# Shared staging rows, later parameter turns, and transfers over 128 partitions with the token group outermost

## The chip, the cores and the metric

One core of a Trainium2 chip runs the whole program: TensorE (PE, with its weight loads PEld), VectorE (DVE), ScalarE (ACT), GpSimd (POOL) and SyncE (SP), and sixteen DMA engines that all queues share. DMAs are issued by SP, ACT and POOL, each in its own order. The metric is the device time of one execution in microseconds. Before the change the median of three runs is 953.67 us (948.99, 953.67, 957.39).

## What is computed

Forward and backward of a gated mix of two branches over L = 2048 tokens of D = 448 channels, all in bf16. `u` is the input, `G` the gradient of the output:

```python
g = sigmoid((u * gate_w).sum(-1, keepdims=True))
a = S4(u)      # y = irfft(rfft(u, 2L) * rfft(K, 2L))[:L] + u * Dskip,  K[d, l] = Re sum_n C dB exp(dt A l)
b = MLP(u)     # relu(u @ w1 + b1)**2 @ w2 + b2
out = g * a + (1 - g) * b
# returned: out, and the gradients of u, A, B, C (real and imaginary), log_dt, Dskip, w1, b1, w2, b2, gate_w
```

## The kernel before, in words

The FFTs are matmuls in two steps of 64 with a turn through DRAM between them. Three sequences are transformed forward: `u` into `gd[0]`, `DA = g * G` into `gd[1]` and the convolution kernel into `gd[2]`. Three products are transformed back through `hd[0]`, `hd[1]`, `hd[2]`. A tile framework gives every engine a fixed order of instructions and sets the semaphores; `tc.issue_after(x)` only puts an instruction behind `x` on its own engine.

**Start (0 to 58 us).** `U` and `G` are held as 128 partitions x 16 tokens: partition 32 g + p holds tokens 64 p + 16 g to 64 p + 16 g + 15, for four groups g of 32 partitions. Eight DMAs load `U` (L398 to L401; each one group of 32 partitions, eight tokens or 7,168 B a row), four load `G` (L410, L411; 14,336 B a row), alternating between SP and ACT. Behind them on SP stand six DMA transposes of the parameters (L420 to L422, the "parameter turns"), the constants `M2`, `MI`, `Etw`, `sel`, and three small loads. `fwd1` (L219 to L241) runs eight steps: four matmuls, their evacuation by ACT and DVE into a staging row of [128, 4, 448], and two stores of 224 KB into `gd`, one from POOL (`q2`) and one from SP. `u` rotates through four staging rows in `F17`, `DA` through six in `R32`. Then `s1_load` (L498) reads `gd` back turned and `fwd2` (L247) makes the spectra with `M2`.

**First inverse (58 to 213 us).** `spectrum`, `powers` (L617; it stores its records to `rec_d` from ACT) and `inv1p` fill `hd[0]`. Four calls of `load_hs` (L316) read it back: each reads 896 KB by two DMAs of 64 partitions, one on ACT and one on SP, 256 rows of 1,792 B each. 160 small matmuls (L713) sum them into the gradient of the convolution kernel, which goes to `dk_d` (L726) and comes back as `DK` (L733). Every chunk of the middle part needs `DK`.

**Middle (213 to 630 us).** Fourteen chunks of parameter gradients, with the MLP's matmuls between them.

**End (630 to 946 us).** Row blocks and weight gradients of the MLP (`grad_w2`, `grad_w1`, whose rows POOL loads at L1148), products of spectra, `inv1` into `hd[1]` and `hd[2]`, eight more calls of `load_hs`, all on SP, into a ring of three buffers that also takes the spectra (`load_sx`, on SP too), `inv2` (L322) and the stores of `out` (L1367, from POOL) and of the gradient of `u` (L1391, SP and ACT), four DMAs of 32 partitions for each of four steps. `G` is loaded a second time at L1267.

The lines that say which DRAM dimension is outermost, in `load_hs` and in the store of `dk_d`:

```python
src = bass.AP(tensor=hd, offset=(8 * hp + 2 * q) * D, ap=[[64 * D, 64], [16 * D, 4], [1, 2 * D]])                       # L318
bass.AP(tensor=dk_d, ..., ap=[[st_ * na * D, 16 // st_], [16 * na * D, 4], [1, D]])   # L726; 16 // st_ is 16, for one piece 8
```

Of the kernel before, what the change touches and what calls it, by code (L numbers as in the profile page):

```python
# [163 lines left out]
class Ker:  # L164
    def __init__(self, tc, pool, psum):
        self.tc = tc
        self.nc = tc.nc
        self.pool = pool
        self.psum = psum
        self.evac_i = 0  # L170
        self.st_i = 0
        self.st_more = []
        self.q2 = tc.nc.gpsimd
        self.pair_i = 0
        self.pairs3 = True
        self.act_only = False
        self.stage_i = 0
        self.dma_i = 0
        self.n = 0
# [39 lines left out]
    def fwd1(self, rhs, gd, stage, act_first=0):  # L219
        nc = self.nc  # L220
        for hh in range(2):
            for q in range(4):
                self.act_only = 4 * hh + q < act_first
                st = stage[self.stage_i % len(stage)]
                self.stage_i += 1
                for j2 in range(2):
                    ps = self.pair()
                    for jj in range(2):
                        self.last_f1 = nc.tensor.matmul(ps[jj][:, 0:D], lhsT=self.F1[:, hh * 128:(hh + 1) * 128], rhs=rhs(q * 4 + j2 * 2 + jj), start=True, stop=True)
                    ev = self.evac2(st[:, 2 * j2:2 * j2 + 2, :], ps)  # L230
                    if self.act_only:
                        self.last_ev = ev
                    elif ev.ins.engine == mybir.EngineType.DVE:
                        self.last_dv = ev
                j0base = 32 * hh + q * 4
                for g2 in range(2):
                    dst = bass.AP(tensor=gd, offset=(j0base + 16 * g2) * 64 * D, ap=[[D, 64], [64 * D, 4], [1, D]])
                    d = (self.q2 if g2 == 0 else nc.sync).dma_start(dst, st[g2 * 64:(g2 + 1) * 64])
                    if g2 == 0:
                        last = d  # L240
        return last  # L241

    def load_s1(self, gd, q, s1, queue=None):
# [70 lines left out]
            nc.scalar.dma_start(dst, st[:])  # L314

    def load_hs(self, hd, q, hs, both=False):  # L316
        for hp in range(2):
            src = bass.AP(tensor=hd, offset=(8 * hp + 2 * q) * D, ap=[[64 * D, 64], [16 * D, 4], [1, 2 * D]])  # L318
            last = (self.nc.scalar if both and hp == 0 else self.nc.sync).dma_start(hs[64 * hp:64 * hp + 64].rearrange("p g x d -> p g (x d)"), src)
        return last  # L320

    def inv2(self, hs, q, x, hp, ps, more=()):  # L322
# [12 lines left out]
def kernel(ctx, tc, A_u, A_A_re, A_A_im, A_B_re, A_B_im, A_C_re, A_C_im, A_log_dt, A_Dskip,  # L335
# [31 lines left out]
    K = Ker(tc, pool, psum)  # L367


    def tl(ap2d, g):  # L370
        return bass.AP(tensor=ap2d.tensor, offset=ap2d.offset + 16 * g * D, ap=[[64 * D, 32], [1, LT * D]])

    def flat(ap):
        return ap.rearrange("p t d -> p (t d)")
# [20 lines left out]
    gw_bc = const.tile([P, D], bf16, name="gw_bc")  # L395
    nc.sync.dma_start(gw_bc[:], gate_w.partition_broadcast(P))
    load_const("F1BD", nc.scalar)
    for h in range(2):  # L398
        for g in range(NG):
            src = bass.AP(tensor=u2.tensor, offset=u2.offset + (16 * g + 8 * h) * D, ap=[[64 * D, 32], [1, 8 * D]])  # L400
            (nc.sync if g % 2 == 0 else nc.scalar).dma_start(flat(U[32 * g:32 * g + 32, 8 * h:8 * h + 8]), src)  # L401
    G_.dma_start(bass.AP(tensor=dk_d, offset=512 * D, ap=[[2 * D, 128], [1, 2 * D]]), nc.inline_tensor(np.zeros((128, 2 * D), ml_dtypes.bfloat16), name="c_zero").ap())
    ldb = const.tile([P, D], bf16, name="ldb")
    G_.dma_start(ldb[:], A_log_dt.partition_broadcast(P))
# [2 lines left out]
    G_.dma_start(prow[FT:FT + 3], A_log_dt[0:384].rearrange("(t p) -> t p", p=P))  # L407
    G_.dma_start(prow[FT + 3:FT + 4, 0:64], A_log_dt[384:448].rearrange("(t p) -> t p", p=64))
    G_.dma_start(prow[0:FT], B_b1.rearrange("(t p) -> t p", p=P))
    for g in range(NG):  # L410
        (nc.sync if g % 2 == 0 else nc.scalar).dma_start(flat(G[32 * g:32 * g + 32]), tl(G2, g))  # L411
    prm = K.t("X16", [P, 8192])
    raw = {}
    o = 0
# [1 line left out]
    def carve(n):  # L416
        nonlocal o
        o += n
        return prm[:, o - n:o]
    for nm, src in (("Ar", A_A_re), ("Ai", A_A_im), ("Br", A_B_re), ("Bi", A_B_im), ("Cr", A_C_re), ("Ci", A_C_im)):  # L420
        r = carve(2 * D).rearrange("p (h d) -> p h d", h=2)
        nc.sync.dma_start_transpose(out=r, in_=src)  # L422
        raw[nm] = r
    load_const("M2", nc.sync)
    for nm in ("MI", "Etw", "sel"):
        load_const(nm, nc.sync)
    K.M2, K.MI, K.Et = ct["M2"], ct["MI"], ct["Etw"]
    sel = ct["sel"][:].rearrange("p (k m) -> p k m", k=4)
    DB = K.t("D16", [P, LT, D])
    ident = const.tile([P, P], bf16, name="ident")  # L430
    make_identity(nc, ident[:])
# [10 lines left out]
    K.F1 = ct["F1BD"]  # L442
    RA = K.t("R32", [P, 16384])
    Fs = K.t("F17", [P, 8704])
    stage = [[b[:, 1792 * i:1792 * i + 1792].rearrange("p (a d) -> p a d", d=D) for i in range(k)] for b, k in ((Fs, 4), (RA, 6))]
    K.fwd1(lambda j: U[:, j, 0:D], gd[0], stage[0], 5)
    u_ev, u_dv, u_f1 = K.last_ev, K.last_dv, K.last_f1
    s32 = const.tile([P, LT], fp32, name="s32")
    s_b = const.tile([P, LT], bf16, name="s_b")
    g_b = const.tile([P, LT], bf16, name="g_b")  # L450
# [17 lines left out]
    SB = K.t("S25", [P, 12800])  # L468
    turn = SB[:, 4096:12288].rearrange("p (k a l) -> p k a l", k=4, a=DT)

    def transposed(src, spill):
        nonlocal nti
        for t2 in range(LT // 2):
            ps = K.ps(NT[4 + nti % 2], [P, DT, 2 * P], bf16)
            nti += 1
            for tt in range(2):
                for dt in range(DT):
                    sv = src[:, 2 * t2 + tt, dt * P:dt * P + DSZ[dt]]
                    for h in range(1 if dt < 3 else 2):
                        T_.transpose(ps[64 * h:64 * h + DSZ[dt], dt, tt * P:tt * P + P], sv, ident[:], tile_position=(0, 64 * h))  # L480
            cp = S.copy if t2 % 2 == 0 else V.tensor_copy
            lb, k = t2 // 2, t2 % 2
            cp(turn[:, lb % 3, :, 256 * k:256 * k + 256], ps[:])
            if k == 1:
                G_.dma_start(bass.AP(tensor=spill, offset=lb * P * 2048, ap=[[2048, P], [1, 2048]]), turn[:, lb % 3].rearrange("p a l -> p (a l)"))
# [5 lines left out]
    V.tensor_copy(b1_f[:], ps[:])  # L491
    ld4 = b1_f[:, FT:FT + 4]

    lf1 = K.fwd1(lambda j: DA[:, j, :], gd[1], stage[1])
    SX, SY = prm, K.t("Y16", [P, 8192])
    s1r = [b[:, 3584 * i:3584 * i + 3584].rearrange("p (a d) -> p a d", d=D) for b in (SY, SX) for i in range(2)]

# [55 lines left out]
    for q in range(2):  # L553
        l11 = s1_load(1, q)
    with tc.issue_after(u_f1.ins):
        transposed(U, UT_d)
    for t in range(LT):
        V.tensor_scalar(out=DB[:, t, :], in0=G[:, t, :], scalar1=omg32[:, t:t + 1], scalar2=None, op0=ALU.mult)
    ps = K.ps("S", [P, 512])
# [57 lines left out]
    def powers(gr):  # L617
# [20 lines left out]
        for k in range(NLEV):  # L638
            dst = xs[..., 2] if k == 0 else ys[..., 1] if k == 2 else lx[..., (1, 8, 9, 10).index(k)] if k in (1, 8, 9, 10) else ly[..., k - 3]
            S.copy(dst.rearrange("p c t w -> p t c w"), x)  # L640
            if k < NLEV - 1:
# [5 lines left out]
        nc.scalar.dma_start(bass.AP(tensor=rec_d, offset=4 * gr * P * RS, ap=[[RS, P], [P * RS, nch], [1, RS]]), R)  # L647


    spw = K.t("K28", [P, 4, 4, 2, D])  # L650
# [19 lines left out]
    for q in range(4):  # L670
        if q < 3:
            if q > 0:
                spectrum(0, q + 1)
            ls1 = spectrum(1, q + 1) or ls1
        for h in range(2):
            pr = prd[(2 * q + h) % 3]
            K.cprod(pr, spw[:, 2 * (q % 2) + 1], spw[:, 2 * (q % 2)], h)
            K.inv1p(pr, 2 * q + h, hd[0])
        if q == 0:
            with tc.issue_after(f10.ins):  # L680
                transposed(DB, DBT_d)
        if q < 2:
            powers(q + 2)
    with tc.issue_after(ls1.ins):
# [578 lines left out]
        sx = [load_sx(0, q) for q in range(3)]  # L1263

    Gt = K.t("Y16", [P, LT, D])
    for g in range(NG):
        nc.sync.dma_start(flat(Gt[32 * g:32 * g + 32]), tl(G2, g))  # L1267
    brs = [RT[:, 10752 + 1792 * i:12544 + 1792 * i].rearrange("p (h x d) -> p h x d", h=2, x=2) for i in range(3)]
    nb = 0

# [35 lines left out]
    for j in range(FT):  # L1306
        grad_w2(j)
        if j == 8:
            for g in range(NG):
                with tc.issue_after(last_s1.ins):  # L1310
                    nc.sync.dma_start(U[32 * g:32 * g + 32, :, 0:D], tl(u2, g).rearrange("p (t d) -> p t d", d=D))
    for j in range(JS):
        grad_w1(j, NB)

# [23 lines left out]
    for q in range(4):  # L1338
# [23 lines left out]
        V.tensor_copy(sl(dg_b), sl(dg))  # L1362
        V.tensor_tensor(out=sl(ds_b), in0=sl(dg_b), in1=sl(gp), op=ALU.mult)
        V.tensor_copy(sl(ds32), sl(ds_b))
        for g in range(NG):
            dst = bass.AP(tensor=o0.tensor, offset=o0.offset + (16 * g + 2 * q) * D, ap=[[64 * D, 32], [8 * D, 2], [1, 2 * D]])
            G_.dma_start(dst, ao[32 * g:32 * g + 32].rearrange("p (h x) d -> p h (x d)", h=2))  # L1367
    param_grads(2)
    param_grads(3)
    GU = K.t("K28", [P, LT, D])  # L1370
# [2 lines left out]
    for q in range(4):  # L1373
        hs = hsn
        if q < 3:
            hsn = load_hs(2, q + 1)
        xo = dxq[2 + q] if q < 2 else oq[q - 2]
        for x in range(2):
            ps = K.pair()
            l0l = 2 * q + x  # L1380
            for hp in range(2):
                t = l0l + 8 * hp
                S.activation(dgt[:, hp], ident[:], ACT.Copy, scale=ds32[:, t:t + 1])
            for hp in range(2):
# [4 lines left out]
        for g in range(NG):  # L1389
            dst = bass.AP(tensor=o1.tensor, offset=o1.offset + (16 * g + 2 * q) * D, ap=[[64 * D, 32], [8 * D, 2], [1, 2 * D]])  # L1390
            K.dma().dma_start(dst, xo[32 * g:32 * g + 32].rearrange("p (h x) d -> p h (x d)", h=2))  # L1391
# [50 lines left out]
```

## Time and profile before

| what | value |
|---|---|
| median of three runs | 953.67 us |
| the profiled execution's own time / span | 947.82 / 945.7 us |
| busy: PE / DVE / ACT / POOL | 713.5 / 670.9 / 586.5 / 192.2 us |
| mean granted TensorE clock | 0.836 |
| DMA, mean over the span | 196 GB/s, 184.98 MB |
| issues of `hd` into `R` on SP: count, size, median to landing | 16, 448 KB, 6.0 us |

The page cuts the span into 40 slices of 23.6 us and gives, for each, the busy share of every engine and the mean busy share of the sixteen DMA engines in tenths; the chain of waits goes back from the last instruction to whatever released each step; the view of one source line gives its instructions, their time from issue to landing and who waited for them. "SPq" is the queue of SP's DMA issues.

### The profile page before, as it was taken

The numbers are of one execution on the slowest core, as the hardware profiler recorded it, in microseconds if no ns is written. First come the engines' busy times: TensorE is split into PE (matmuls) and PEld (weight loads), VectorE is DVE, ScalarE is ACT, GpSimd is POOL, SyncE is SP. The second block draws the span as 40 slices with busy tenths as digits, with TensorE's granted clock in tenths as the row PEclk, the third lists the DMA queues.
The fourth block names the chain that finished last, engine by engine and source line by source line (L and its number), as shares of the span: only waits on it lengthen the run. The fifth ranks groups of instructions, "written<-read, shape, count | busy, mean of one in ns | idle before, by whom it ended". The sixth has DMA issues, their size and how long they took to land.

```text
span 945.7 us, 19001 instructions
## 1 busy us (share of the span) xinstructions
PE 713.5 (75%) x7657; PEld 342.6 (36%) x7657; DVE 670.9 (71%) x1152; ACT 586.5 (62%) x936; POOL 192.2 (20%) x327
## 2 busy tenths in 40 slices
PE   3346564635978888887898887988869889768985
PEld 1112221214344443434453443543323245423443
DVE  4388986696399999999887899944248671297800
ACT  3345757825998868789676855655237646437553
POOL 2141000112202121121202311232300022433310
PEclk9687565667969998899957999989968889869999
DMA  8987395896626667444844867279999994889431
GB/s 191 266 254 263 120 354 225 306 309 193 146 62 124 151 143 137 111 110 117 198 85 117 218 149 189 79 193 288 378 295 279 295 292 146 228 236 278 144 110 44
DMA packets 161887, 184.98 MB, mean 196 GB/s; under 512 B 90963, under 2 KB 137464, under 8 KB 160872
## 3 DMA queue, kind: packets, MB, share of 16 engines
q1 hardware_dynamic: 111958, 82.38, 35.2%
q0 software_dynamic: 20480, 61.51, 20.3%
q10 hardware_dynamic: 29362, 39.88, 12.9%
q8 instruction: 60, 0.98, 0.5%
q14 instruction: 27, 0.22, 0.1%
HBM read 90.58 MB, written 73.13 MB: 173 GB/s over the span
## 4 chain that ended last, share of the span: by engine, by line
PE 24%; issue 19%; ACT 18%; DMA 17%; DVE 14%; POOL 5%; SPq 2%; ACTq 1%; POOLq 0%; DVEq 0%
PE psN L1021 4%; PE psF L1159 3%; DMA S<-rT_d 2%; ACT R L917 2%; SPq L422 2%; PE psX L844 2%; POOL dhT_d L1097 2%; ACT S L591 2%; DMA hd<-st 1%; PE psN L584 1%; DMA D<-hd 1%; ACT R L871 1%; DMA out_dram<-S 1%; DMA dk_d<-st 1%; DMA U<-in_A_u_dram 1%
## 5 line engine op out<-in xcount | busy, mean ns | idle before, releaser
L1159 PEld LDWEIGHTS <-S 128*128 128x128 bf16 x448 | 44.2, 104 | 63.0 <-issue 20.5
L933 DVE TENSOR_TENSOR P<-R 128x2048 bf16<-128x2048 bf16 x42 | 49.5, 1217 | 23.5 <-ACT R L917 20.6
L917 ACT CAST R<-psF 128x1024 bf16<-128x1024 f32 x56 | 57.5, 1027 | 11.2 <-PE psF L913 11.2
L1021 PE MATMUL psN<-D,S 128*128 128x448 bf16 x208 | 52.0, 382 | 6.4 <-ACT S L591 6.3
L1159 PE MATMUL psF<-U,S 128*128 128x448 bf16 x224 | 51.4, 380 | 2.1 <-ACT S L1154 2.0
L584 PE MATMUL psN<-S,U 128*128 128x512 bf16 x132 | 41.0, 429 | 8.3 <-ACT F L589 4.7
L913 PE MATMUL psF<-R,S 64*32 64x256 bf16 (+1 forms) x1344 | 38.4, 299 | 8.5 <-DMA R<-Y 3.2
L1084 PE MATMUL psN<-S,U 128*128 128x512 bf16 x126 | 36.9, 410 | 7.5 <-ACT D L1089 6.9
L773 DVE TENSOR_TENSOR X<-X,F 128x512 bf16<-128x512 bf16 (+1 forms) x70 | 37.5, 536 | 4.5 <-ACT F L807 2.6
L207 DVE CAST K<-psN 128x448 bf16<-128x448 f32 x36 | 21.7, 620 | 26.5 <-PE psN L255 26.2
L784 DVE TENSOR_TENSOR K<-K,F 128x2048 bf16<-128x2048 bf16 (+3 forms) x42 | 36.4, 866 | 5.6 <-ACT F L812 4.0
L1153 PEld LDWEIGHTS <-S 128*128 128x128 bf16 x448 | 29.8, 102 | 26.4 <-issue 10.0
L1097 POOL DMA_DIRECT2D dhT_d<-D x28 | 20.2, 722 | 90.8 <-DVE D L1096 90.4
L785 DVE TENSOR_TENSOR F<-K,F 128x2048 bf16<-128x2048 bf16 (+3 forms) x42 | 35.9, 855 | 2.7 <-ACT F L814 2.7
L784 DVE TENSOR_TENSOR Y<-Y,F 128x2048 bf16<-128x2048 bf16 (+3 forms) x42 | 36.3, 864 | 1.6
L774 DVE TENSOR_TENSOR F<-X,F 128x512 bf16<-128x512 bf16 (+1 forms) x70 | 36.9, 527 | 0.6
L787 DVE TENSOR_TENSOR K<-K,F 128x2048 bf16<-128x2048 bf16 (+3 forms) x42 | 36.3, 865 | 1.3
L787 DVE TENSOR_TENSOR Y<-Y,F 128x2048 bf16<-128x2048 bf16 (+3 forms) x42 | 36.3, 864 | 1.3
L785 DVE TENSOR_TENSOR F<-Y,F 128x2048 bf16<-128x2048 bf16 (+3 forms) x42 | 35.9, 854 | 0.2 <-ACT F L814 0.2
L1021 PE MATMUL psN<-S,D 128*128 128x448 bf16 x168 | 35.5, 360 | 0.0
L1354 DVE SCALAR_TENSOR_TENSOR F<-psN,Y 128x448 bf16<-128x448 f32 x16 | 9.9, 618 | 36.1 <-PE psN L329 36.1
L883 ACT COPY M<-psX 128x1024 bf16<-128x1024 bf16 x26 | 26.5, 1018 | 13.7 <-PE psX L882 13.3
(378 smaller groups left out, 1944.1 us busy)
## 6 DMA issues: line engine op xcount, KB each, us to landing
sp<-K ACTq DMA_DIRECT2D x8, 896.0 KB, 6.4
hd<-st ACTq DMA_DIRECT2D x16, 448.0 KB, 3.0
dhT_d<-D POOLq DMA_DIRECT2D x28, 256.0 KB, 5.3
R<-sp SPq DMA_DIRECT2D x8, 896.0 KB, 8.9
S<-rT_d POOLq DMA_DIRECT2D x14, 512.0 KB, 5.2
R<-hd SPq DMA_DIRECT2D x16, 448.0 KB, 6.0
S<-dhT_d POOLq DMA_DIRECT2D x14, 512.0 KB, 4.3
rec_d<-F ACTq DMA_DIRECT2D x2, 1920.0 KB, 9.1
```

Source lines behind the costliest of these rows:

```text
L584: T_.matmul(ps[:], lhsT=w1w[:, dt, j * P:j * P + P], rhs=ub[:, dt], start=(dt == 0), stop=False, skip_group_check=True)
L773: V.tensor_tensor(out=hi4, in0=lo, in1=bcast_dims(pr, [0, (None, n), 1]), op=ALU.mult)
L774: V.tensor_tensor(out=Vv.rearrange("p (x a r) -> p x a r", x=2 * W2, r=2), in0=lo, in1=bcast_dims(pi, [0, (None, n), 1]), op=ALU.mult)
L784: V.tensor_tensor(out=hi, in0=lo, in1=bcast_dims(pr, [0, (None, n // 2), 1]), op=ALU.mult)
L785: V.tensor_tensor(out=Vv.rearrange("p (x a q) -> p x a q", x=rows, q=2), in0=lo, in1=bcast_dims(pi, [0, (None, n // 2), 1]), op=ALU.mult)
L787: return V.tensor_tensor(out=T4[:, :, :, n:2 * n], in0=T4[:, :, :, n:2 * n], in1=V4, op=ALU.add)
L913: T_.matmul(psz[32 * ii:32 * ii + m, t, 256 * s:256 * s + 256], lhsT=DKc[64 * t:64 * t + 64, s, g, 2 * ii:2 * ii + 1 + par].rearrange("p i ...
L917: S.copy(zb[:, :, :, gg].rearrange("p s t n -> p t s n"), psz[:].rearrange("p t (s n) -> p t s n", s=2))
L933: lastp = V.tensor_tensor(out=pr.rearrange("p s t g n -> p s t (g n)"), in0=zv, in1=(xb if r == 0 else rev_dim(xb, 2)), op=ALU.mult)
L1021: lastm = T_.matmul(ps[:, 0:D], lhsT=hblk[j][:, P * tt:P * tt + P], rhs=ws[:, j, :], start=(w == 1 and j == 0), stop=(j == FT - 1))
L1097: G_.dma_start(bass.AP(tensor=dhT_d, offset=2 * p_ * P * L + 512 * lb, ap=[[L, P], [P * L, 2], [1, 512]]), hb)
L1159: lastm = T_.matmul(ps[:, 0:width], lhsT=hh[:, t, :], rhs=(DB2[:, t, :] if w == 0 else U[:, t, 0:D + 1]), start=(t == 0), stop=(t == LT - 1))
```

## The change

1. The two lists of staging rows become one list of ten (four in `F17`, six in `R32`); `u` uses rows 0 to 7, `DA` rows 8, 9 and 0 to 5.
2. The parameter turns and the loads of `M2`, `MI`, `Etw` and `sel` are put behind the last store of `u` on SP.
3. `DA`'s second stores go from SP to ACT (`q3`).
4. `U` is loaded by four DMAs of four tokens over all 128 partitions, `G` by two of eight tokens (both times). `load_hs` uses four DMAs over 128 partitions instead of two over 64; the stores of `out` and of `u`'s gradient use two DMAs of 128 partitions instead of four of 32.
5. The evacuations of `u`'s transposes all go to ACT (they alternated between ACT and DVE), and the four stores of `rec_d` move from ACT to POOL.

```diff
@@ fwd1
-                    d = (self.q2 if g2 == 0 else nc.sync).dma_start(dst, st[g2 * 64:(g2 + 1) * 64])
+                    d = (self.q2 if g2 == 0 else self.q3).dma_start(dst, st[g2 * 64:(g2 + 1) * 64])
@@ load_hs
-        for hp in range(2):
-            src = bass.AP(tensor=hd, offset=(8 * hp + 2 * q) * D, ap=[[64 * D, 64], [16 * D, 4], [1, 2 * D]])
-            last = (self.nc.scalar if both and hp == 0 else self.nc.sync).dma_start(hs[64 * hp:64 * hp + 64].rearrange("p g x d -> p g (x d)"), src)
+        for g in range(4):
+            src = bass.AP(tensor=hd, offset=(2 * q + 16 * g) * D, ap=[[8 * D, 2], [64 * D, 64], [1, 2 * D]])
+            last = (self.nc.scalar if both and g % 2 == 0 else self.nc.sync).dma_start(hs[:, g].rearrange("p x d -> p (x d)"), src)
@@ main function
-    def tl(ap2d, g):
-        return bass.AP(tensor=ap2d.tensor, offset=ap2d.offset + 16 * g * D, ap=[[64 * D, 32], [1, LT * D]])
+    def tl(ap2d, t0, n):
+        return bass.AP(tensor=ap2d.tensor, offset=ap2d.offset + t0 * D, ap=[[16 * D, NG], [64 * D, 32], [1, n * D]])
...
-    for h in range(2):
-        for g in range(NG):
-            src = bass.AP(tensor=u2.tensor, offset=u2.offset + (16 * g + 8 * h) * D, ap=[[64 * D, 32], [1, 8 * D]])
-            (nc.sync if g % 2 == 0 else nc.scalar).dma_start(flat(U[32 * g:32 * g + 32, 8 * h:8 * h + 8]), src)
+    for h in range(4):
+        (nc.sync if h % 2 == 0 else nc.scalar).dma_start(flat(U[:, 4 * h:4 * h + 4]), tl(u2, 4 * h, 4))
...
-    for g in range(NG):
-        (nc.sync if g % 2 == 0 else nc.scalar).dma_start(flat(G[32 * g:32 * g + 32]), tl(G2, g))
+    for h in range(2):
+        (nc.sync if h % 2 == 0 else nc.scalar).dma_start(flat(G[:, 8 * h:8 * h + 8]), tl(G2, 8 * h, 8))
...
-    stage = [[... for i in range(k)] for b, k in ((Fs, 4), (RA, 6))]
-    K.fwd1(lambda j: U[:, j, 0:D], gd[0], stage[0], 5)
+    stage = [... for b, k in ((Fs, 4), (RA, 6)) for i in range(k)]
+    K.fwd1(lambda j: U[:, j, 0:D], gd[0], stage, 5)
+    with tc.issue_after(u_st.ins):       # the turns and M2, MI, Etw, sel, moved here from above
...
-            cp = S.copy if t2 % 2 == 0 else V.tensor_copy
+            cp = cps[t2 % 2]             # (S.copy, S.copy) for U, (S.copy, V.tensor_copy) for DB
...
-    lf1 = K.fwd1(lambda j: DA[:, j, :], gd[1], stage[1])
+    K.q3 = nc.scalar
+    lf1 = K.fwd1(lambda j: DA[:, j, :], gd[1], stage)
+    K.q3 = nc.sync
...
-        nc.scalar.dma_start(bass.AP(tensor=rec_d, ...), R)
+        G_.dma_start(bass.AP(tensor=rec_d, ...), R)
...
-    for g in range(NG):
-        nc.sync.dma_start(flat(Gt[32 * g:32 * g + 32]), tl(G2, g))
+    for h in range(2):
+        nc.sync.dma_start(flat(Gt[:, 8 * h:8 * h + 8]), tl(G2, 8 * h, 8))
...
-        for g in range(NG):
-            dst = bass.AP(tensor=o0.tensor, offset=o0.offset + (16 * g + 2 * q) * D, ap=[[64 * D, 32], [8 * D, 2], [1, 2 * D]])
-            G_.dma_start(dst, ao[32 * g:32 * g + 32].rearrange("p (h x) d -> p h (x d)", h=2))
+        for h in range(2):
+            dst = bass.AP(tensor=o0.tensor, offset=o0.offset + (8 * h + 2 * q) * D, ap=[[16 * D, NG], [64 * D, 32], [1, 2 * D]])
+            G_.dma_start(dst, ao[:, 2 * h:2 * h + 2].rearrange("p x d -> p (x d)"))
...
@@ the same edit at the store of o1, on the queues of K.dma()
```

More of the change, by code (lines that the diff above doesn't have):

```diff
@@ L173, in __init__ @@
         self.q2 = tc.nc.gpsimd
+        self.q3 = tc.nc.sync
         self.pair_i = 0
@@ L237, in fwd1 @@
                     dst = bass.AP(tensor=gd, offset=(j0base + 16 * g2) * 64 * D, ap=[[D, 64], [64 * D, 4], [1, D]])
-                    d = (self.q2 if g2 == 0 else nc.sync).dma_start(dst, st[g2 * 64:(g2 + 1) * 64])
+                    d = (self.q2 if g2 == 0 else self.q3).dma_start(dst, st[g2 * 64:(g2 + 1) * 64])
                     if g2 == 0:
                         last = d
+                    else:
+                        self.last_st = d
         return last
@@ L419, in carve @@
         return prm[:, o - n:o]
[L420 to L428, printed above, removed]
     DB = K.t("D16", [P, LT, D])
@@ L444 @@
     Fs = K.t("F17", [P, 8704])
-    stage = [[b[:, 1792 * i:1792 * i + 1792].rearrange("p (a d) -> p a d", d=D) for i in range(k)] for b, k in ((Fs, 4), (RA, 6))]
-    K.fwd1(lambda j: U[:, j, 0:D], gd[0], stage[0], 5)
-    u_ev, u_dv, u_f1 = K.last_ev, K.last_dv, K.last_f1
+    stage = [b[:, 1792 * i:1792 * i + 1792].rearrange("p (a d) -> p a d", d=D) for b, k in ((Fs, 4), (RA, 6)) for i in range(k)]
+    K.fwd1(lambda j: U[:, j, 0:D], gd[0], stage, 5)
+    u_ev, u_dv, u_f1, u_st = K.last_ev, K.last_dv, K.last_f1, K.last_st
+    with tc.issue_after(u_st.ins):
+        for nm, src in (("Ar", A_A_re), ("Ai", A_A_im), ("Br", A_B_re), ("Bi", A_B_im), ("Cr", A_C_re), ("Ci", A_C_im)):
+            r = carve(2 * D).rearrange("p (h d) -> p h d", h=2)
+            nc.sync.dma_start_transpose(out=r, in_=src)
+            raw[nm] = r
+        load_const("M2", nc.sync)
+        for nm in ("MI", "Etw", "sel"):
+            load_const(nm, nc.sync)
+        K.M2, K.MI, K.Et = ct["M2"], ct["MI"], ct["Etw"]
+    sel = ct["sel"][:].rearrange("p (k m) -> p k m", k=4)
     s32 = const.tile([P, LT], fp32, name="s32")
@@ L469, with transposed @@
     turn = SB[:, 4096:12288].rearrange("p (k a l) -> p k a l", k=4, a=DT)
-    def transposed(src, spill):
+    def transposed(src, spill, cps):
         nonlocal nti
@@ L555 @@
     with tc.issue_after(u_f1.ins):
-        transposed(U, UT_d)
+        transposed(U, UT_d, (S.copy, S.copy))
     for t in range(LT):
@@ L646, in powers @@
                 x, y = y, halves(cur[1 - k % 2])
-        nc.scalar.dma_start(bass.AP(tensor=rec_d, offset=4 * gr * P * RS, ap=[[RS, P], [P * RS, nch], [1, RS]]), R)
+        G_.dma_start(bass.AP(tensor=rec_d, offset=4 * gr * P * RS, ap=[[RS, P], [P * RS, nch], [1, RS]]), R)
     spw = K.t("K28", [P, 4, 4, 2, D])
@@ L680 @@
             with tc.issue_after(f10.ins):
-                transposed(DB, DBT_d)
+                transposed(DB, DBT_d, (S.copy, V.tensor_copy))
         if q < 2:
@@ L1310 @@
                 with tc.issue_after(last_s1.ins):
-                    nc.sync.dma_start(U[32 * g:32 * g + 32, :, 0:D], tl(u2, g).rearrange("p (t d) -> p t d", d=D))
+                    nc.sync.dma_start(U[32 * g:32 * g + 32, :, 0:D], bass.AP(tensor=u2.tensor, offset=u2.offset + 16 * g * D, ap=[[64 * D, 32], [D, LT], [1, D]]))
     for j in range(JS):
@@ L1388 @@
             brq.append(load_br(1, q + 3))
-        for g in range(NG):
-            dst = bass.AP(tensor=o1.tensor, offset=o1.offset + (16 * g + 2 * q) * D, ap=[[64 * D, 32], [8 * D, 2], [1, 2 * D]])
-            K.dma().dma_start(dst, xo[32 * g:32 * g + 32].rearrange("p (h x) d -> p h (x d)", h=2))
+        for h in range(2):
+            dst = bass.AP(tensor=o1.tensor, offset=o1.offset + (8 * h + 2 * q) * D, ap=[[16 * D, NG], [64 * D, 32], [1, 2 * D]])
+            K.dma().dma_start(dst, xo[:, 2 * h:2 * h + 2].rearrange("p x d -> p (x d)"))
     dlog_b = const.tile([P, 4], bf16, name="dlog_b")
```

## The prediction

> **What bounds the kernel now.** I read the table of stretches first, then the chain of waits, then the source lines the change touches. The stretches (us, busy of PE, PEld, DVE, ACT and POOL, granted clock, DMA share, GB/s):
>
> ```profile
> 24.00:58.00 34.00, 16.87 (x98) 7.61 (x99) 16.69 (x38) 15.65 (x27) 6.59 (x11) 0.75 0.96 263
> ...
> 192.00:213.00 21.00, 7.91 (x111) 4.23 (x113) 20.11 (x31) 4.09 (x7) 3.60 (x6) 0.67 0.98 308
> 213.00:260.00 47.00, 35.35 (x491) 19.61 (x488) 24.54 (x36) 35.89 (x52) 11.69 (x19) 0.85 0.64 168
> ...
> 741.00:770.00 29.00, 25.61 (x144) 10.92 (x144) 17.66 (x28) 16.50 (x29) 5.31 (x10) 0.76 0.94 278
> 770.00:812.00 42.00, 38.20 (x285) 21.21 (x283) 12.54 (x13) 21.51 (x32) 8.71 (x17) 0.96 0.62 206
> ...
> 835.00:888.00 53.00, 43.09 (x269) 17.70 (x269) 46.12 (x127) 27.57 (x62) 16.85 (x31) 0.79 0.83 234
> ```
>
> The three places where the change works, the start, the read of `hd[0]` at 192 and the end from 741, have a DMA share of 0.83 to 0.98. There the sixteen DMA engines are the scarce thing. The chain of waits (start, us, what), at the start and at 187:
>
> ```profile
> 19.22 5.42 SPq L422
> ...
> 33.26 3.73 DMA gd<-F
> 37.09 0.92 ACT F L216
> ```
>
> ```profile
> 187.45 4.98 DMA hd<-st
> 193.26 12.35 DMA D<-hd
> ...
> 211.60 11.00 DMA dk_d<-st
> 225.78 6.49 DMA K<-dk_d
> ```
>
> First: `u`'s fifth step waits for a staging row whose store stands behind the turns on SP. The view of the `fwd1` stores says who paid (us, times), and that of `load_hs` whom it held:
>
> ```profile
>   DVE F L207: 14.5, 1
>   ACT F L216: 13.9, 1
> ```
>
> ```profile
>   PEld L713: 19.4, 3
>   PE psN L713: 18.1, 3
> ...
> DMA to landing us min/median/max: 4.8/6.6/14.7
> ```
>
> Second: the read of `hd[0]` (issued at 192.6, last landing at 212.7) holds the sums L713, and they hold `DK`.
>
> **The row that decides.** The trace's semaphore records give the increments that each DMA makes on landing. Nearly all make 16. The two `dk_d` stores on SP whose DRAM pattern begins with 8 (218.1 and 218.8 us; 32 partitions on the SBUF side) make 9, those that begin with 16 make 16, one-row DMAs make 2, and the 14-row store at 939.5 makes 15. So on SP and ACT a short transfer shows one more increment than its outermost count: eight rows outermost are served by eight engines, one by one. The changed patterns begin with 2 (`load_hs`) and with 4 (`U`, `G`, `out`, `u`'s gradient); before, the smallest among them was 32. I take 2 and 4 engines. Which engines these are no record says: the ends are the same ones every time, or a fresh set for each DMA. I take the same ones, since nothing in the trace shows a rotation, and keep the other end as a rival.
>
> The Trainium skill ("DMA: Bandwidth & Descriptors", section "Why a DMA increments its semaphore by 16 and not by 1") says that the engine count is the largest number up to 16 that divides the slowest dimension of both sides, and that SP and ACT use the lowest-numbered ones. The rows agree with the first half; the second no row shows, and with it the first end would hold.
>
> The price of one engine comes from the packet records. Their times add up to the page's DMA share, so an engine serves one packet at a time: at the median 41 ns for 896 B, 74 to 86 ns for 1,792 B (by queue), 144 ns (lowest tenth) for 3,584 B, 272 ns for 7,168 B.
>
> **Part by part.**
>
> *Read of `hd[0]`.* 4 calls x 4 DMAs x 128 packets of 1,792 B on 2 engines is 1,024 packets each, x 74 to 80 ns = 76 to 82 us. SP's half and ACT's half share the two engines, so two queues do not help. `w2`, `UT` and the records use the same engines for some 5 us. From 192.6 + 2.5 to the first byte, the end lies at 271 to 282 instead of 212.7: +58 to +69. DVE (20.1 of 21 us busy) finishes its tables meanwhile, but in 213:260 it is busy 24.5 of 47 us, so finishing early buys little; the hidden layer that fills PE there needs `w1`, queued on SP behind these reads. The `dk_d` stores, 11.0 us beside the weights' loads now, should land some 5 us sooner. I take +60, bounds +50 to +69.
>
> *Reads of `hd[1]` and `hd[2]`.* A call is 4 x 64 packets an engine x 74 to 80 ns = 19 to 20.5 us on two engines; now 6 to 13 us. All eight stand on SP, in one order. The other traffic of 741:888 is, by engine, 27 + 26 + 21 + 44 us of busy share (812:835 has 0.89), less 26 for these reads (16 DMAs x 16 packets x 0.1 us under load) and 11 for the output stores (32 x 4 x 0.087): 81 us, which shares the two engines. With a quarter more for that, 24 us a call. Walking it: call (1,0), issued at 741.4, lands at about 775 instead of 750 (shared fully there), so its `inv2` (754.6 now) moves 21 to 25. Calls (1,1) and (1,2) hide behind `grad_w2`, where PE is busy 38.2 of 42 us. From (1,3) on, five calls follow at 24 us: 862, then 892, 916, 940 and 964, against a last need at 872.5: +90. At 19 us a call it is +65, at 30 us +120. The count confirms it: two engines have 81 + 156 (eight calls) + 19 (`u`'s gradient: 8 DMAs x 32 packets x 74 ns on four engines) = 256 us to carry, where 147 us stood. PE's order is fixed, so the late `grad_w1` steps wait too. I take +90.
>
> *Start.* Removed: the 13.9 us wait, and the turns ahead of `u`'s stores. Added: `U` is 4 x 32 packets x 144 ns = 18.4 us on four engines, all landed by about 24 instead of 15.4; `G` is 2 x 32 x 272 ns = 17.4 us behind it, landed at about 41 instead of 24.5. `u`'s transform then ends near 35 instead of 42.7, but `DA` starts at `G`'s landing, about where it starts now (41.3). On SP the turns now take their 16.5 us (13.1 to 29.7) from about 35, with four of their engines backed up, and `M2` lands at 52 to 58. `fwd2` starts at 57.5 now and needs it: -6 to +10, taken as 0. The gain is there and `G` and the turns are late next.
>
> *Second read of `G`, stores of `out`.* 17.4 us on four engines on SP where some 5 stood, in a stretch with DMA share 0.97: 0 to +13, taken as +4, nearest to the early landing (706) against the need (755). The POOL stores are half as many issues of 0.56 us; POOL's queue made 16 increments for every shape, so its engine count cannot be read: -2 to +5, taken as 0.
>
> *`rec_d` from POOL; `DA`'s stores from ACT; evacuations to ACT.* The landing of `rec_d` (9.07 us in the chain) stays, POOL pays four issues of about 1 us; behind them wait the `DBT_d` stores, which nobody needs soon: -2 to +6, taken as +1. Eight ACT issues of 0.4 us and four copies of 1.02 us fall into ACT's idle time at 57.9 to 68.6 (9.4 us before L539): 0, +3 if uncovered. `powers(0)` now waits for `DA`'s rows in `F17`, as the memsets of `R32` do already (4.0 us before 65.8): 0 to +4, taken as 0.
>
> Sum: 60 + 90 + 0 + 4 + 0 + 1 = +155 on the profiled 947.8, which is 1,103. The median of the runs shown lies 5.9 above the profiled run: 1,109, given as 1,110. Bounds: -10 to +41 from the small parts, +115 to +189 from the reads: 1,059 to 1,184.
>
> **Rivals.**
>
> *Faster: the reads keep sixteen engines or rotate* (0.09). The nine-increment rows are stores; no load with a short outermost count is in the trace. If each load takes fresh engines, four DMAs of 4.9 + 2.4 us in parallel land as now (6.6 at the median), and the start is all that is left: the wait of 13.9 us less the turns behind `u` (16.5 us from about 28 end at 45, `M2` by 50, 7 before 57.5), so -7 to -14: 943. It decides where a call keeps about eight engines or more; with eight, the reads already cost +10 in the first inverse.
>
> *Only the first read costs* (0.08). If the fixed order was set with the long reads in view and puts `grad_w1` ahead of `inv2`, PE's 58 us behind 888 cover most of the end: 5.9 + 947.8 + 60 + 15 = 1,029. Against it: the other loads queue on the same two engines.
>
> *Every wide transfer slows* (0.08). While two engines are backed up, each 16-engine DMA lands with its slowest part; POOL's row loads at L1148 then come late even where PE does not wait for `inv2`, and 30 us a call or more gives +120 to +150 at the end: 1,140 to 1,190.
>
> *Nothing changes* (0.03): gains and losses meet within 1%, about what a measurement of this kernel can tell from no change.
>
> **How the numbers follow.** The main case has 0.72. Its own range is 1,059 to 1,184. To leave out no more than 2 in 10, the range goes down to 1,020 (the second rival) and ends at 1,185. Of the first rival's -7 to -14 a third or more lies within 1% (9.5 us): faster 0.05, within 1% 0.07 with the last rival, slower 0.88.
>
> **What would show it.** Right: `load_hs` DMAs with 3 increments and those of `U` with 5; a stretch of some 60 us with a low DMA share after 192, with PE L713 waiting for `D<-hd` and `P<-hd`; `psN` L329 waiting for `R<-hd` from 850 on; no wait of ACT for `gd<-F` before 40. Wrong: 16 increments there, a landing of `hd` under 10 us, or a DMA share over 0.9 in that stretch.

## The result and the profile after

The changed kernel takes 1148.72 us at the median of four runs (1145.56 to 1152.38) against 952.75 us for the kernel before in the same session (948.99 to 957.39): the ratio is 1.2055, with a 95% interval of 1.199 to 1.2121. The profiled execution took 1149.55 us (span 1147.7), 201.7 us more than the profiled one before. That one lies 4.9 us below the median, so by the medians the change costs 196.0.

The view of `load_hs` first, that is L322 of the changed kernel (operation, tiles, count, then the shortest, median and longest issue in ns, first and last start, and below it who waited, in us and times):

```profile
L322 SPq DMA_DIRECT2D R<-hd x32: 486/4320/8635, 839.8 to 1057.3; - x32
...
L322 SPq DMA_DIRECT2D P<-hd x4: 8734/9114/9153, 219.9 to 247.9; - x4
L322 ACTq DMA_DIRECT2D P<-hd x4: 4202/9156/15267, 220.0 to 248.7; - x4
...
  PE psN L717: 77.4, 8
  ACT F L818: 61.0, 1
  PE psN L332: 42.5, 9
  ACT S L1158: 23.7, 1
```

The same view of the kernel before, L319:

```profile
L319 SPq DMA_DIRECT2D P<-hd x2: 587/624/661, 193.9 to 194.5; - x2
...
  PE psN L713: 18.1, 3
  PE psN L329: 2.5, 1
```

Two things are to be seen. The sums (L717, L713 before) now wait 77.4 us for `hd[0]`, where they waited 18.1, and the second inverse (L332) 42.5 us for the later calls, where it waited 2.5. And the *issue* of one such DMA holds SP or ACT for some 9.1 us from the third of each queue on, up to 15.3, where it took 0.6 to 0.85. The trace's records give each DMA 3 increments; they give those of `U`, `G` and `u`'s gradient 5, and those of `out`, issued by POOL, 16.

The table of stretches (us, busy of PE, PEld, DVE, ACT and POOL, granted clock, DMA share, GB/s) has the start, the read of `hd[0]`, what follows it, and the end:

```profile
24.00:58.00 34.00, 18.82 (x92) 8.28 (x93) 20.82 (x56) 16.93 (x29) 6.23 (x10) 0.90 0.71 179
199.00:289.00 90.00, 18.63 (x124) 7.10 (x126) 32.82 (x54) 5.34 (x9) 3.36 (x6) 0.54 0.30 96
289.00:330.00 41.00, 33.72 (x468) 17.70 (x462) 10.72 (x11) 31.55 (x46) 11.64 (x19) 0.87 0.52 128
840.00:930.00 90.00, 59.55 (x372) 27.95 (x369) 24.28 (x34) 34.15 (x55) 11.01 (x20) 0.74 0.46 157
930.00:1020.00 90.00, 51.53 (x296) 22.24 (x292) 30.79 (x80) 25.00 (x48) 21.41 (x35) 0.75 0.47 143
1020.00:1090.00 70.00, 28.83 (x140) 9.19 (x139) 21.56 (x56) 17.02 (x40) 5.89 (x11) 0.59 0.26 85
```

Before, the DMA engines were 0.62 to 0.98 busy in these places; now it is 0.26 to 0.47 in the reads and at the end, while the other engines wait for them. The read of `hd[0]` takes 89.2 us (199.2 to 288.4) instead of 20.1, at a DMA share of 0.30. Its 2,048 packets of 1,792 B take 79.5 ns on average by the packet records, 163 us in all: two engines that serve them one at a time need 81 of the 89 us. The page's slices show the same, tenths of the sixteen engines and GB/s; the ninth slice, 230 to 258 us, reads 1 tenth and 49 GB/s, which is two engines at 24.5. In that slice the records have two of these packets under way for 91% of the time and three or four for the rest, though the two queues together had four DMAs or more in flight:

```profile
DMA  4797568215364565556466576988852656323132
GB/s 122 186 330 263 229 248 295 78 49 160 95 143 113 120 141 119 118 133 151 95 139 187 144 127 176 283 284 244 268 196 80 216 165 200 104 92 103 63 120 69
```

The chain of waits at that place (start, us, what) consists of the reads alone, their issue on ACT and then the landing of the last. Before, 12.4 us stood here, and the `dk_d` store's 11.0 behind it:

```profile
210.80 9.17 ACTq L322
...
224.25 15.27 ACTq L322
239.55 9.16 ACTq L322
248.75 39.66 DMA P<-hd
...
299.68 6.22 DMA K<-dk_d
```

To follow where the time came from, I read the same instructions in each trace. The table gives how much later (us) each starts than in the kernel before, for the changed kernel and for six of the experiments below:

| instruction | before at | after | e1 | e2 | e3 | e7 | e8 | e9 |
|---|---|---|---|---|---|---|---|---|
| last matmul of `u` in `fwd1` | 41.6 | -4.5 | -3.9 | +0.6 | -15.7 | -16.0 | -15.9 | -16.0 |
| first matmul of `fwd2` | 57.5 | +20.1 | +22.4 | +1.3 | +0.9 | +0.4 | +5.0 | +7.8 |
| last store of `hd[0]` | 187.5 | +6.7 | +9.5 | +2.9 | -11.6 | -11.5 | -9.8 | -16.5 |
| first chunk that uses `DK` | 232.7 | +73.6 | +9.1 | +68.9 | -12.4 | -12.4 | -10.0 | -17.1 |
| load of the convolution kernel (`xs`) | 627.5 | +79.4 | +14.8 | +75.5 | -7.5 | -13.7 | -5.3 | -13.8 |
| first matmul of the end's weight gradients | 694.1 | +95.5 | +30.0 | +75.3 | -9.2 | +2.6 | -6.4 | -14.7 |
| last matmul of these | 937.1 | +200.9 | +24.3 | +169.3 | -10.0 | -3.7 | -3.7 | -15.9 |

Each column comes from one trace, and the trace of the kernel before is the quick one named above. For the changed kernel the steps between the rows are +6.7 (start), +66.9 (read of `hd[0]`), +5.8 (middle), +16.1 (second read of `G`) and +105.4 (end): 200.9.

### The profile page after: what moved, and what is told of

It reads as the page before. It is cut to its first block, busy times and chain, and to the rows that moved or that the text cites. A ratio compares the mean times of both kernels' runs of the same rounds, so it can differ in the third digit from the quotient of the medians.

```text
span 1147.7 us, 19007 instructions
## 1 busy us (share of the span) xinstructions
PE 747.0 (65%) x7657; PEld 348.6 (30%) x7657; DVE 668.5 (58%) x1148; ACT 591.8 (52%) x940; POOL 191.0 (17%) x323
## 3 DMA queue, kind: packets, MB, share of 16 engines
q1 hardware_dynamic: 109610, 80.55, 28.2%
## 4 chain that ended last, share of the span: by engine, by line
DMA 30%; PE 25%; ACT 16%; DVE 10%; issue 8%; ACTq 5%; SPq 5%; POOL 1%; DVEq 0%; POOLq 0%
DMA R<-hd 7%; DMA R<-sp 5%; PE psN L1025 5%; ACTq L322 4%; DMA K<-in_grad_out_dram 4%; DMA P<-hd 3%; SPq L322 3%; DMA gd<-P 2%; PE psN L588 2%; PE psX L848 2%; ACT R L921 2%; PE psF L1163 2%; PE psF L917 1%; PE psX L1163 1%; DMA R<-br_d 1%
## 5 line engine op out<-in xcount | busy, mean ns | idle before, releaser
L1163 PEld LDWEIGHTS <-S 128*128 128x128 bf16 x448 | 45.5, 107 | 89.1 <-issue 37.0
L1163 PE MATMUL psF<-U,S 128*128 128x448 bf16 x224 | 54.5, 397 | 15.3 <-ACT S L1158 15.2
L818 ACT ACTIVATE F<-recy 128x640 bf16<-128x640 bf16 (+2 forms) x30 | 19.7, 700 | 61.0 <-DMA P<-hd 61.0
L588 PE MATMUL psN<-S,U 128*128 128x512 bf16 x132 | 43.2, 449 | 8.4 <-ACT F L593 4.8
L332 PE MATMUL psN<-R,cb_Etw 64*32 64x448 bf16 x128 | 20.1, 466 | 42.5 <-DMA R<-hd 42.5
L1158 ACT ACTIVATE S<-psS 128x1024 bf16<-128x1024 bf16 x24 | 24.8, 1031 | 35.4 <-DMA R<-hd 23.7
L1088 PE MATMUL psN<-S,U 128*128 128x512 bf16 x126 | 39.3, 434 | 5.4 <-ACT D L1093 5.4
L313 PE MATMUL psN<-P,cb_MI 64*128 64x448 bf16 x128 | 28.0, 412 | 21.0 <-ACT st L207 7.4
L270 DVE TENSOR_TENSOR F<-R,K 128x1792 bf16<-128x1792 bf16 x8 | 8.7, 1089 | 54.3 <-DMA R<-br_d 48.5
L258 PEld LDWEIGHTS <-M 128*64 128x64 bf16 x192 | 14.1, 131 | 80.8 <-issue 53.3
L1240 DVE TENSOR_TENSOR X<-U,X 128x256 f32<-128x256 bf16 (+1 forms) x24 | 9.2, 420 | 50.1 <-ACT X L1247 49.8
L788 DVE TENSOR_TENSOR Y<-Y,F 128x2048 bf16<-128x2048 bf16 (+3 forms) x42 | 36.3, 865 | 1.6
```

Of the source, the lines that this page charges most:

```text
L588: T_.matmul(ps[:], lhsT=w1w[:, dt, j * P:j * P + P], rhs=ub[:, dt], start=(dt == 0), stop=False, skip_group_check=True)
L788: V.tensor_tensor(out=hi, in0=lo, in1=bcast_dims(pr, [0, (None, n // 2), 1]), op=ALU.mult)
L1088: T_.matmul(ps[:], lhsT=w2Tw[:, jp, dt, j % 2], rhs=dblk[:, dt], start=(dt == 0), stop=False, skip_group_check=True)
L1163: lastm = T_.matmul(ps[:, 0:width], lhsT=hh[:, t, :], rhs=(DB2[:, t, :] if w == 0 else U[:, t, 0:D + 1]), start=(t == 0), stop=(t == LT - 1))
```

## The experiments

Every ratio is to the kernel before, run in the same session, with its 95% interval.

**e1, the changed kernel with `load_hs` as before.**

```diff
-        for g in range(4):
-            src = bass.AP(tensor=hd, offset=(2 * q + 16 * g) * D, ap=[[8 * D, 2], [64 * D, 64], [1, 2 * D]])
+        for hp in range(2):
+            src = bass.AP(tensor=hd, offset=(8 * hp + 2 * q) * D, ap=[[64 * D, 64], [16 * D, 4], [1, 2 * D]])
```

> The changed kernel with load_hs as before (two DMAs of 64 partitions, DRAM pattern beginning with 64); all the rest of the change stays. Theory A (two engines serve a pattern that begins with 2): the read of hd[0] takes 20 us again instead of 89, the reads of hd[1] and hd[2] stop holding inv2; about 67 us and 85 to 105 us go, so 975 to 1,000 us against 1,148.7. Theory B (the cost lies elsewhere, in U, G, the stores of out and the new order of the start): less than 60 us go, above 1,085 us. Between them: a mixture, whose share the stage times tell.

971.5 us, ratio 1.0154 (1.0085 to 1.0223): 177 us less than the changed kernel. The read of `hd[0]` takes 20.2 us again, with 16 increments a DMA and a DMA share of 1.01. The stretch, and the view of L322:

```profile
202.00:223.00 21.00, 8.68 (x122) 4.84 (x126) 19.52 (x29) 3.46 (x6) 3.16 (x5) 0.70 1.01 318
```

```profile
L322 SPq DMA_DIRECT2D R<-hd x16: 512/524/1782, 772.0 to 897.1; - x16
...
  PE psN L717: 9.2, 3
  PE psN L332: 7.1, 4
```

The long issues are gone with the two-engine pattern, as is ACT's wait of 61 us.

**e2, the kernel before with the new `load_hs` alone** (the reverse edit).

> The kernel before with the new load_hs alone (four DMAs of 128 partitions, DRAM pattern beginning with 2). Theory A: +67 us in the first inverse and +85 to +105 at the end: 1,100 to 1,130 us, increments of 3 for each of these DMAs. Theory B: within 60 us of the kernel before, under 1,015 us.

1117.4 us, ratio 1.1702 (1.1637 to 1.1766). The read takes 89.3 us, with 3 increments a DMA. In the table it adds 66.0 up to the first chunk (+2.9 to +68.9), and the end adds 94.0 (+75.3 to +169.3), with every other transfer as before.

**e3, the changed kernel with all its reshaped transfers as before** (`load_hs`, `U`, both reads of `G`, the stores of `out` and of `u`'s gradient). What remains are the ten staging rows, the later turns, and the moves of the evacuations, of `DA`'s stores and of `rec_d`.

```diff
-    for h in range(4):
-        (nc.sync if h % 2 == 0 else nc.scalar).dma_start(flat(U[:, 4 * h:4 * h + 4]), tl(u2, 4 * h, 4))
+    for h in range(2):
+        for g in range(NG):
+            src = bass.AP(tensor=u2.tensor, offset=u2.offset + (16 * g + 8 * h) * D, ap=[[64 * D, 32], [1, 8 * D]])
+            (nc.sync if g % 2 == 0 else nc.scalar).dma_start(flat(U[32 * g:32 * g + 32, 8 * h:8 * h + 8]), src)
...
```

> The changed kernel with every transfer of part 4 as before (U, G twice, load_hs, out, u's gradient); left are the ten shared rows, the later turns, DA's stores on ACT, the evacuations on ACT and rec_d on POOL. Theory A (the loss is the short outermost dimension, the rest is what the first rival of the prediction has left): 940 to 950 us, no wait for gd<-F before 40 us. Theory C (the new order of the start loses too, as the first spectrum 20 us late may say): 955 to 970 us.

940.86 us, ratio 0.9853 (0.9794 to 0.9913); run again in a later session, 936.48 us, 0.984 (0.9797 to 0.9884). The rest of the change is a gain. The view of the `fwd1` stores, who waited for it, us and times:

```profile
  POOL F L623: 6.0, 1
  POOL gd L239: 2.2, 1
```

The two waits of 14.5 and 13.9 us for a staging row, shown of the kernel before, are gone, and `u`'s transform ends 15.7 us sooner. `fwd2` doesn't start sooner (+0.9), but the work behind it is ahead: the last store of `hd[0]` by 11.6 us, the first chunk by 12.4.

**e4, the changed kernel with `load_hs` cut into eight DMAs of 64 partitions a call** instead of four of 128. The packets are those of the change; the outermost count is 64.

```diff
-            src = bass.AP(tensor=hd, offset=(2 * q + 16 * g) * D, ap=[[8 * D, 2], [64 * D, 64], [1, 2 * D]])
+            for hp in range(2):
+                src = bass.AP(tensor=hd, offset=(2 * q + 16 * g + 8 * hp) * D, ap=[[64 * D, 64], [1, 2 * D]])
```

> The changed kernel with load_hs as eight DMAs of 64 partitions (112 KB each, DRAM pattern beginning with 64), twice as many issues as in the changed kernel and the same rows of 1,792 B. Theory A: 16 increments each, the read of hd[0] near 20 to 25 us, within 10 us of the run with load_hs as before. Theory D (the number of issues and the time SP and ACT stand in them is the cost, up to 15 us an issue in the changed kernel): as slow as the changed kernel or slower, 1,149 us and more.

992.06 us, ratio 1.0368 (1.0293 to 1.0444). The read of `hd[0]` takes 22.4 us with 32 issues of 0.44 to 0.84 us and 16 increments each. From the view of its line, L323:

```profile
L323 SPq DMA_DIRECT2D P<-hd x8: 444/445/463, 209.0 to 216.0; - x8
L323 ACTq DMA_DIRECT2D P<-hd x8: 452/452/452, 209.3 to 216.5; - x8
```

The kernel is 157 us faster than the changed one with the same bytes, packets and tile and twice the issues, so neither the split by token group nor the size or the number of the DMAs is the cause. It is 20.6 us above e1, which has a quarter of the issues. That is more than expected, and no run here explains it further.

**e5, the kernel before with each DMA of `load_hs` cut into 62 and 2 partitions.** It tells two readings of the increments apart: the outermost count itself (62 would be served by all sixteen engines), or its largest divisor up to 16 (2).

```diff
+            for p0, n in ((0, 62), (62, 2)):
-            src = bass.AP(tensor=hd, offset=(8 * hp + 2 * q) * D, ap=[[64 * D, 64], [16 * D, 4], [1, 2 * D]])
+                src = bass.AP(tensor=hd, offset=(8 * hp + 2 * q + 64 * p0) * D, ap=[[64 * D, n], [16 * D, 4], [1, 2 * D]])
```

> The kernel before with each DMA of load_hs cut by partitions into 62 and 2; the pattern of the large one begins with 62, not a short count. Theory A1 (the engines are as many as the largest number up to 16 that divides the outermost count: 2 for 62): increments of 3, the read of hd[0] near 85 us, 1,100 to 1,130 us in all, like the run with the new load_hs alone. Theory A2 (only a count below 16 limits, as the prediction read its rows): 16 increments for the piece of 62, the read of hd[0] at 20 to 26 us, 955 to 975 us.

1110.74 us, ratio 1.1652 (1.1596 to 1.1709). The pieces of 62 partitions make 3 increments and the read takes 94.3 us, as long as with an outermost 2. The view of that line, L320, with the same columns as above:

```profile
L320 SPq DMA_DIRECT2D P<-hd x4: 1044/9123/17183, 223.2 to 242.7; - x4
L320 ACTq DMA_DIRECT2D P<-hd x4: 1123/9156/18344, 225.1 to 244.7; - x4
...
  PEld L714: 79.7, 4
  PE psN L714: 77.5, 4
```

The number of engines is the largest divisor, not the count. The Trainium skill ("DMA: Bandwidth & Descriptors", section "Why a DMA increments its semaphore by 16 and not by 1") states this rule for both sides of a DMA, and these 3 increments agree with it.

**e6, the changed kernel with the read of `hd[0]` on SP alone**: does the second queue bring anything, and what does it cost ACT?

```diff
-        lhs = K.load_hs(hd[0], q, hss[q], True)
+        lhs = K.load_hs(hd[0], q, hss[q])
```

> The changed kernel with all sixteen DMAs of the read of hd[0] on SP, none on ACT. Theory A (the two engines set the read, whichever queue feeds them): the read stays at 82 to 92 us; ACT is free for the tables that waited 61 us for it, but they were not late last, so the total stays within 10 us of the changed kernel. Theory D (ACT standing in its issues is what costs): 20 us or more below the changed kernel. If two queues overlapped something on an engine, the read grows beyond 92 us.

1144.0 us, ratio 1.2015 (1.1958 to 1.2072). The read takes 88.2 us on one queue and 89.2 on two: both queues feed the same two engines. An issue on SP then takes 4.6 us instead of 9.1, half; that this is because its predecessors no longer share the engines with another queue is likely, not shown.

```profile
L322 SPq DMA_DIRECT2D P<-hd x8: 4062/4631/7661, 232.4 to 269.7; - x8
```

With ACT free of the issues, the second chunk's generating matmuls (L848) end 6.3 us sooner than in the changed kernel. By the eighth chunk the two traces are level (506.7 us in both); later e6 is ahead again, 10 us at the end, but in the total the medians differ by 4.7 us and the intervals of the two overlap.

**e7, e1 with the first loads of `U` and `G` as before too** (the second read of `G` and the stores stay on four engines).

> The changed kernel with load_hs and the first loads of U and G as before; the second read of G and the stores of out and u's gradient stay as changed (outermost count 4). Against the run with load_hs alone put back (971.5) it tells the price of U and G at the start: theory A, by the stage times (the dk_chunk 9 us late there, 12 early with all put back), 15 to 25 us, so 947 to 957 us. If the start does not matter to the end, 965 to 972 us.

952.08 us, ratio 0.9968 (0.9928 to 1.0007). Against e1 the loads of `U` and `G` at the start are worth 19.4 us, and against e3 the second read of `G` and the stores cost 11.2, both across two sessions in which the kernel before differs by 2.6. Read from one trace each: in the table the step from the load of `xs` to the first weight gradient is +16.3 here, +15.2 in e1 and +16.1 after, but -0.2 in e2 and -1.7 in e3, where `G` is read the old way. Part of it is made up later.

**e8, only the rows and the turns on the kernel before**: e3 with `DA`'s second stores on SP, the evacuations alternating and `rec_d` on ACT, as they were.

```diff
-    K.q3 = nc.scalar
+    K.q3 = nc.sync
-        transposed(U, UT_d, (S.copy, S.copy))
+        transposed(U, UT_d, (S.copy, V.tensor_copy))
-        G_.dma_start(bass.AP(tensor=rec_d, ...), R)
+        nc.scalar.dma_start(bass.AP(tensor=rec_d, ...), R)
```

> The kernel before with the ten shared rows and the later turns alone (DA's stores on SP, evacuations alternating, rec_d on ACT, all transfers as before). If the gain of 15 us of the run with all transfers put back comes from the wait for a staging row, it stays: 936 to 946 us. If it comes from the moves to ACT and POOL, 948 to 956 us.

943.55 us, ratio 0.9923 (0.9889 to 0.9956). The 15.9 us of `u`'s transform are all there, and 10.0 of them at the first chunk. The three small moves together add some 5 us to it: e3 lies 15.1 and 14.7 us below the kernel before in its two sessions, e8 9.9. The intervals of e8 and the first e3 overlap, those of e8 and the second just don't, so this share is likely, not shown.

**e9, e10, e12: can the start of e3 be mended further?** e9 puts `DA`'s second stores on POOL (`K.q3 = G_`), since ACT issued them late, in e3 until 55 us. e10 puts VectorE's block of parameter work behind `DA`'s last evacuation. e12 does both.

```diff
-    K.q3 = nc.scalar
+    K.q3 = G_                                    # e9, e12
-    with tc.issue_after(u_dv.ins):
+    with tc.issue_after(K.last_dv.ins):          # e10, e12
```

> The run with all transfers put back, with DA's second stores on POOL instead of ACT. There ACT stood 9.3 us before an evacuation (47.75 us), after two store issues that themselves waited for DVE. Theory F (the issue in ACT's order holds ACT back, and with it the last steps of DA's transform): DA's transform ends about 8 us sooner and the total falls by 3 to 8 us, to 933 to 938. Theory G (the first spectrum waits for gd[0], read on SP behind the turns, at 58 us, so DA's transform is covered): 938 to 943, no change.

> The run with all transfers put back, with DVE's parameter block put behind DA's last evacuation on DVE instead of u's. Theory H (DVE's block, which waits for the turns, holds up DA's evacuations and is itself not late): 3 to 8 us less, 933 to 938. Theory I (the block is on the path to the powers tables; behind DA it comes later): 3 to 10 us more, 944 to 951.

> Both of the last two edits together, on the run with all transfers put back. If F and H hold, 930 to 936 us; if G and I hold, 944 to 951, the parameter block being the price.

> The run with all transfers put back once more, on the same chip as the last three, to compare them with it: 938 to 944 us, 1 to 2% below the kernel before.

They took 935.58 us (0.9824, 0.9785 to 0.9863), 937.53 (0.9824, 0.9779 to 0.987) and 929.65 (0.9756, 0.9711 to 0.9802); e3 beside them took 936.48. In e9 `DA`'s transform ends 11.8 us sooner than in that run of e3, and yet `fwd2` starts at 65.3 instead of 58.9. Its chain of waits leads through the turns into the parameter work:

```profile
30.87 1.45 SPq L448
...
38.57 4.61 SPq L448
43.22 12.07 DMA X<-in_A_C_im_dram
```

L448 are the turns, now behind `u`'s stores. The last of them lands after 12.1 us, in that run of e3 after 6.0. `fwd2` itself waits 17.8 us for its read of `gd`: that read is issued at 50.5, no later than in e3 (51.0), but lands after 14.7 us instead of 7.8. The DMA share is 1.10, 1.12 and 1.02 in 30:45, 45:55 and 55:65; in e3 it is 0.86 in the last of these. So with `DA`'s stores sooner, the DMA engines themselves, full until 65 us, are probably late next. Neither edit alone can be told from e3. Together they are 6.8 us below it, with intervals that just touch; that they gain is likely, not shown. Where e12 gains is not shown here. It is faster than both kernels.

## Why the prediction was right, and where its terms were off

The sign, the place and the mechanism held: the reads of `hd` fell to two engines. Foretold were 155 us, measured are 201.7 (196.0 by the medians). The signs that the prediction named are all in the trace: 3 and 5 increments, a stretch with a low DMA share after 192 in which the sums wait for `D<-hd` and `P<-hd`, waits of the second inverse after 850, and none of ACT for a staging row.

| term | foretold | measured |
|---|---|---|
| start | 0 (-6 to +10) | +20.1 at `fwd2`, +6.7 at the last store of `hd[0]` |
| read of `hd[0]` | +60 (50 to 69) | +66.9 |
| middle | not in the sum | +5.8 |
| second read of `G` | +4 (0 to 13) | +16.1 |
| reads of `hd[1]` and `hd[2]`, end | +90 (65 to 120) | +105.4 |
| `rec_d`, `DA`'s stores, evacuations | +1 (-2 to +13) | not separate in this table; e3 and e8 make a gain of some 5 likely |

*Read of `hd[0]`.* "76 to 82 us" on two engines was right: 81 of packet time in 89.2. The read is 69.1 us longer, the upper end of the "+58 to +69" that was worked out, of which +60 was taken. What was missed is that the issuing engines are held too. The prediction had the table work finish meanwhile. But ACT stood in its issues from 200 to 258 us and its part of the tables waited 61.0 us. Between 289 and 330 us ACT is therefore the busiest but PE, 31.6 of 41 us. e6 takes ACT out of the issues: its second chunk is some 6 us ahead, but not its first (+75.0 against +73.6), and the lead is gone by the eighth. So this holding does not explain the +66.9, and a lasting cost of it is not shown.

*End.* "24 us a call" was right for the reads alone: in e2 the last five calls landed 23.6 us apart on average, and the reads cost 94.0 against 90 foretold; calls two and three hid behind other work, as the walk had it. In the changed kernel it was too little: there the last five landed 28.2 us apart, and from the first issue to the last landing the eight calls took 29.1 to 44.3. The other 11 us are the difference between the changed kernel and e2 in this stage. The reshaped stores, the later loads or both may be behind them; e7 doesn't part them, and no run here does. In e1 and e7, with the same stores and loads but quick reads, this stage is 5.7 and 6.3 us shorter than before, so no such loss is seen without the slow reads.

*Second read of `G`.* The packets were priced rightly where they can be told apart (280 ns on average in the first read of `G`, against 272), but the second read is not alone: its two DMAs landed after 17.6 and 41.5 us, and the first two loads of spectra queued behind it on SP after 31.5 and 34.1, where before the first three took 21.6 to 28.5. The working weighed the landing of `G` against the need for `G`, and not what is queued behind it. e1, e7, e2 and e3 agree on some 16 us for it.

*Start.* Foretold was the landing of `U` at 24, of `G` at 41 and of `M2` at 52 to 58; measured are 29.3, 45.7 and 73.6. The chain of waits of the changed kernel there (start, us, what):

```profile
2.77 42.88 DMA K<-in_grad_out_dram
...
55.12 3.04 SPq L443
...
61.79 7.69 DMA X<-in_A_C_im_dram
...
69.62 7.86 DMA Y<-gd
```

`G` on four engines is the first link, the turns (L443) the next, the reading back of `gd` the last: "`G` and the turns are late next" was the right order, with 5 us too little on `G`. The turns began at 50 us instead of 35, and the reading of `gd` behind them, 7.9 us, was not counted. `fwd2` came 20.1 us late, outside the foretold -6 to +10; 13 of that are made up again at the last store of `hd[0]`, which no step of the prediction foresaw. That the start nearly kept its term is luck. The price of the four-engine loads at the start is 19.4 us (e7 against e1), hidden in the sum by the gain of the staging rows.

*Middle.* The +5.8 can't be told from the spread of this stretch: it moved by -1.3 (e7), +4.9 (e3) and +5.7 (e1) in kernels with the same middle part, and in the second trace of e3, the very same kernel, by -2.2 (granted clock 0.90 in 249:616, against 0.87 in 248:622 of the first).

*The rivals.* That the reads rotate over the engines is excluded: 81 of 89 us of work for two engines, and mostly two packets under way however many DMAs are in flight. But the gain which that rival foretold without the slow transfers, -7 to -14, is what e3 shows: 15.1 and 14.7 us below the kernel before. "Only the first read costs" falls by e2's 94 us at the end. "Every wide transfer slows" foretold the total best (1,140 to 1,190), and part of what it names happened (the spectra's and `G`'s landings, the calls of 29 us and more). Its cause isn't the sixteen-engine DMAs in general, though: the sixteen-increment stores of `out` landed in 6.0 to 8.6 us throughout, and POOL's row loads, which this rival named, in 3.9 to 8.6 us between 840 and 1020 (3.9 to 10.0 in 741:888 before). Loads on SP behind the slow reads did slow: that of the last spectrum, issued at 898.7, took 24.2 us (8.9 before).

*The reading of the increments.* "Its outermost count" was too narrow: by e5 it is the largest divisor up to 16. For 2, 4, 8 and 14 both say the same, so no term of the sum changes.

## What to carry to other kernels

Before a DMA is reshaped, look at the outermost count on both of its sides, at its largest divisor up to 16 (62 counts as 2), and at the increments of the nearest DMA in the trace: with one more than 2, 4 or 8 increments, that many engines carry it, and 128 partitions on the SBUF side don't help when the DRAM side begins with 2. When one edit of a change is slow, run the rest without it: here e3 is 1.5% faster than before, under a change that is 20% slower, and e12 2.4%. What is queued behind a slow DMA belongs into its price; what is held on its issuing engine has to be looked at too, though here no lasting cost of it is shown.

## What the runs showed of the hardware that was not expected

- The issue of a DMA that two engines carry holds the issuing engine itself: 9.1 us at the median on SP and on ACT, up to 15.3, and 4.6 us where SP alone issues. By the records, each issue from the third on ended when two earlier DMAs of that queue were still under way, and on each queue the first six landings were some 9.3 us apart. ACT's compute waits for that as well (61.0 us).
- 62 partitions are carried by two engines (3 increments), at 94.3 us for a read that 64 partitions make in 20.1.
- Two engines moved 49 GB/s in the ninth slice, with packets of 1,792 B.
- The same DRAM shape with an outermost 4 made 5 increments from SP and ACT and 16 from POOL (the stores of `out`).
- Where PE was busy 18.6 of 90 us (199:289) the granted clock was 0.54, where it was busy 28.8 of 70 (1020:1090) it was 0.59; over the whole run it was 0.779 against 0.836 before.
